# A sign bit cleared on ScalarE, one addition of epsilon, and other positions for helper work in a fused attention and experts kernel

## Chip, cores and metric

The kernel runs on one core of one Trainium2 chip. The metric is the device time of one execution in microseconds, as the median of some runs. Of the core's engines TensorE (PE) multiplies, VectorE (DVE), ScalarE (ACT) and GpSimd (POOL) do the elementwise work, and SyncE (SP) issues all the DMAs from one queue. Each engine works its own instructions in order.

## What is computed

Three layers follow each other on 2304 tokens of width 512.

```python
# 1. linear attention: batch 4, heads 8, sequence 576, head width 64
q_s = softmax(q, axis=-1); k_s = softmax(k, axis=2)      # sums have 1e-09 added
x = q_s @ (k_s^T @ v)                                    # then (B*S, H*D) = (2304, 512)
# 2. four experts, all used, 512 -> 1024 -> 512
p = domain_probs / (domain_probs.sum(-1) + 1e-09)
x = sum_e p[:, e] * (relu(x @ w1[e]) @ w2[e])
# 3. gated layer, 512 -> 1536 -> 512; w_gate, w_val, w_out come as 64-bit floats
g = x @ w_gate
out = (g * sigmoid(g) * (x @ w_val)) @ w_out
```

## The kernel before

**Numbers.** Every operand of a large product is split into a high and a low half (`split`, L103: ScalarE rounds the high half, VectorE or GpSimd subtracts). `mm3` (L107) makes one product of three matmuls: high by high, high by low, low by high. The hidden products go by seven products of 2 x 2 blocks in place of eight (`chain`, L486; the table PRODUCTS says which of seven prepared columns `xh`, `xl` and weights go together). Between the products, ScalarE copies a bank (`snap`, L503) and VectorE adds it to another (L509, L518, L524).

**Steps.** The tokens are two halves of two batches; a half is cut into block X (512 tokens) and block Y (640 tokens). A unit is 256 hidden columns of one expert (kind "e", 32 units over both halves) or of the gated layer (kind "g", 12 units). A unit and a block make a step, 88 in all. SE = 32 is the first step of the second half's experts, SG = 64 the first gated step, SF = 76 the first gated step of the second half. In the trace step 4 begins at 122.67 us, SE at 499.64, step 36 at 558.74, SG at 893.54 and SF at 1117.68, each read from the first matmul of its weights.

**Weaving.** In step st TensorE makes the hidden block of this step (`stage_h`, 8 positions in kind "e", 14 in kind "g") and the output tiles of the step before (`stage_y`, two advances for each tile of 128 tokens: 8 for X, 10 for Y). `weave` (L754) goes from position to position: first a piece of the hidden block, then DMA stores that have come of age, then the hooks of that position, then as many advances of the output tiles as WEAVE says; what is left of the tiles goes out after the last position. The low half of the hidden block is made on VectorE (L643, L645) at the first positions of the next step.

**Hooks.** All other work hangs on pairs (step, position): the attention of the second half of the batches (`attend`, steps 2 to 29), loading and splitting weights, and these four:

- `decode` (L553) turns the 64-bit weights into 32-bit ones, half a unit's matrix at a time, 36 halves, in DRAM for later. Half n begins at eighth 51 + 12n of a step, so at position 3 and 7 in turn, from step 6 to step 58; two further stages follow two and four positions later. ScalarE scales the low words (L558); VectorE clears the sign bit of the high words (L559), clamps (L561), shifts (L563), puts the sign back (L564) and adds the low words (L566). Two buffers r take turns; the load of half n + 2 is hung behind half n.
- `save_x` (L401), by the table SAVE: TensorE turns the 128 x 128 blocks of a finished sum, ScalarE copies them, SP stores them (`sd`).
- `prepare` (L428), by PREPARE (first step after SE or SG, positions in a step, first position, distance): loads the turned sums, makes the seven columns and their halves, stores them (`pd`); READY loads the finished columns.
- `load_x` and `combine_load` (L415, L421), by LOAD_E: the same for the second half's attention result, straight from DRAM into the columns.

**What sets the order.** In step 2 and later TensorE and ScalarE keep exactly the order in which the program writes their instructions (`ordered`, L779). VectorE, GpSimd and SP get theirs from a scheduler that knows estimated durations and lets a ready instruction of a later place fill a hole. Before step 2 the scheduler orders all engines, and a written list says in which order attention pieces are emitted.

**Epsilon.** In `att_kv` the sum of the key softmax comes from a column of ones behind v, one per head (`ov[:, z, D:]`). Both columns of ones give the same sum in every partition.

The lines of the change:

```python
for z in range(GH):                                                   # L234
    zz = slice(z * D, (z + 1) * D)
    nc.vector.tensor_scalar_add(rs[zz], ov[zz, z, D:], EPS)
...
nc.scalar.activation(lo, lo.bitcast(U32), AF.Copy, scale=2.0 ** -29)  # L558
nc.vector.tensor_scalar(c, hi, 0x7FFFFFFF, None, ALU.bitwise_and)     # L559
```

Of the kernel before, what the change touches and what calls it, by code (L numbers as in the profile page):

```python
# [10 lines left out]
F32 = mybir.dt.float32  # L11
# [3 lines left out]
AF = mybir.ActivationFunctionType  # L15
ALU = mybir.AluOpType
# [3 lines left out]
EPS = 1e-9  # L20
# [7 lines left out]
def attention_experts_swiglu(ctx: ExitStack, tc: tile.TileContext, q, k, v, probs, w1, w2, wg, wv, wo, out):  # L28
# [12 lines left out]
    nc = tc.nc  # L41
    B, H, S, D = q.shape
# [13 lines left out]
    GH = 2  # L56
# [20 lines left out]
    def sbt(tag, shape, name, dt=F32):  # L77
        return sb.tile(shape, dt, tag=tag, name=name, bufs=BUFS[tag])
# [4 lines left out]
    def ps(tag, name):  # L83
        if tag in TURNS:
            TURNS[tag].append(TURNS[tag].pop(0))
            tag = TURNS[tag][0]
        return psp[-1].tile([P, 512], F32, tag=tag, name=name, bufs=BUFS[tag])
# [12 lines left out]
    def f32(ap):  # L100
        return ap.bitcast(F32)
# [15 lines left out]
    def store_later(dst, src):  # L117
        later.append((now[0], dst, src))
# [57 lines left out]
    def load_q(b, g, qt):  # L176
        h = slice(g * GH, (g + 1) * GH)
        nc.sync.dma_start(qt, q[b, h, 0:SM, :].rearrange("h (p c) d -> p h c d", c=C))
        nc.sync.dma_start(rests[b, g][RQ], q[b, h, SM:S, :].rearrange("h r d -> r h d"))
        qin[b, g] = (qt, rests.pop((b, g)))  # L180
# [3 lines left out]
    def W(z):  # L184
        return WAITS[z]

    def att_kv(b, g, tag, tag_m, tag_kv, bank):


        nm = f"{b}{g}"  # L190
        kt, vt, kr, vr = kin.pop((b, g))
        m = sbt(tag_m, [P, 2, P], f"m{nm}")
        kc = kt.rearrange("p h c d -> p c h d")
        nc.vector.tensor_tensor(m.rearrange("p c (h d) -> p c h d", h=GH), kc[:, 0:2], kc[:, 2:4], ALU.max)
        yield W(0), False
        tp = ps(bank, f"ktp{nm}")[:, :2 * P + SR]
        for c in range(2):
            nc.tensor.transpose(tp[:, c * P:(c + 1) * P], m[:, c], ident)
        nc.tensor.transpose(tp[:, 2 * P:], kr[R].rearrange("p h d -> p (h d)"), ident[R, R])
        yield W(1), True  # L200
        mx = sbt("ti", [P, 1], f"mx{nm}")
        nc.vector.tensor_reduce(mx, tp, AX.X, ALU.max)
        yield W(2), False
        mb = ps(bank, f"kmb{nm}")[:, :P]
        nc.tensor.matmul(mb, mx.to_broadcast([P, P]), ident, start=True, stop=True)
        yield W(3), True
        es = sbt(tag, [P, 2, C, GH, D], f"e{nm}") if isinstance(tag, str) else tag
        ek, eqs[b, g] = es[:, 0], es[:, 1]
        mbv = mb.rearrange("p (h d) -> p h d", h=GH)
        nc.vector.tensor_tensor(  # L210
            ek.rearrange("p c h d -> p h c d"), kt, mbv[:, :, None, :].to_broadcast([P, GH, C, D]), ALU.subtract
        )
        nc.vector.tensor_tensor(kr[R], kr[R], mbv[R], ALU.subtract)
        if (b, g) in rests:
            load_q(b, g, kt)
        nc.scalar.activation(ek, ek, AF.Exp)
        nc.scalar.activation(kr[R], kr[R], AF.Exp)
        yield W(4), False
        o = ps(bank, f"kvp{nm}")[:, :GH * D1]
        for c in range(C):  # L220
            nc.tensor.matmul(  # L221
                o, ek[:, c].rearrange("p h d -> p (h d)"), vt[:, c].rearrange("p h d -> p (h d)"),
                start=c == 0, stop=False,
            )
        nc.tensor.matmul(
            o, kr[R].rearrange("p h d -> p (h d)"), vr[R].rearrange("p h d -> p (h d)"), start=False, stop=True
        )
        yield W(5), True
        rs = sbt("ti", [P, 1], f"rs{nm}")
        ov = o.rearrange("p (z e) -> p z e", z=GH)  # L230
        kk = sbt(tag_kv, [P, 2, P], f"kk{nm}", F32R)
        kh, kl = kk[:, 0], kk[:, 1]
        nc.gpsimd.memset(f32(kk), 0.0)
        for z in range(GH):  # L234
            zz = slice(z * D, (z + 1) * D)
            nc.vector.tensor_scalar_add(rs[zz], ov[zz, z, D:], EPS)
        nc.vector.reciprocal(rs, rs)
        for z in range(GH):
            zz = slice(z * D, (z + 1) * D)
            nc.scalar.activation(kh[zz, zz], ov[zz, z, 0:D], AF.Copy, scale=rs[zz])  # L240
            nc.vector.scalar_tensor_tensor(kl[zz, zz], ov[zz, z, 0:D], rs[zz], f32(kh)[zz, zz], ALU.mult, ALU.subtract)
        kvs[b, g] = (kh, kl)
        yield W(6), False
# [309 lines left out]
    def decode(n):  # L553
        what, f, z = DEC[n]
        r = r64.pop(n)
        rv = r[:, 0:2 * NE].rearrange("p (n b) -> p n b", b=2)
        lo, hi, c = rv[:, :, 0], rv[:, :, 1], r[:, 2 * NE:]
        nc.scalar.activation(lo, lo.bitcast(U32), AF.Copy, scale=2.0 ** -29)  # L558
        nc.vector.tensor_scalar(c, hi, 0x7FFFFFFF, None, ALU.bitwise_and)  # L559
        cf = c.bitcast(F32)  # L560
        nc.vector.tensor_scalar(cf, cf, LEAST, MOST, ALU.max, ALU.min)  # L561
        yield
        nc.vector.tensor_scalar(c, c, 3, 0x3FFFFFF8, ALU.logical_shift_left, ALU.bitwise_and)  # L563
        nc.vector.scalar_tensor_tensor(c, hi, -0x40000000, c, ALU.bitwise_and, ALU.bitwise_or)  # L564
        yield
        nc.vector.tensor_tensor(c, c, lo, ALU.add)  # L566
        if (what, f) not in w32:
            w32[what, f] = dram.tile([P, 2 * NE], F32, tag=f"w32_{what}{f}", name=f"w32_{what}{f}")
        store_later(w32[what, f][:, z * NE:(z + 1) * NE], cf)
        yield  # L570
# [142 lines left out]
    def store(hf, t, src):  # L713
# [9 lines left out]

    END = {"e": 7, "g": 13}
    WEAVE = {
        "e": [0, 0, 2, 2, 2, 1, 2],
        "end": [0, 0, 0, 10],
        "g": [0, 0, 0, 0, 2, 0, 0, 0, 0, 0, 2, 2, 10, 13],
    }


# [2 lines left out]


    SAVE = [
        [[(-1, 1), (-1, 3), (-1, 5), (0, 1)], [(2, 1), (2, 3), (2, 5), (2, 7)]],
        [[(-1, 1), (-1, 3), (-1, 4), (0, 0)], [(1, 2), (1, 4), (1, 7), (1, 11)]],
    ]

    LOAD_E = [[(-3, 20), (-2, 3), (-2, 7)], [(-2, 7), (-1, 3), (-1, 6)], [(-1, 6), (0, 3), (0, 6)], [(0, 6), (1, 2), (1, 5)]]

    PREPARE = [[5, 8, 0, 4], [3, 14, 0, 2]]

    READY = [
        [[(-3, 1), (-3, 2), (-3, 3), (-3, 4), (-3, 5), (-3, 6), (-3, 7)], [(-1, 1), (-1, 2), (-1, 3), (-1, 4), (-1, 5), (-1, 6), (-1, 7)]],
# [20 lines left out]
    def at(step, pos, fn, *a):  # L767
        plan.setdefault(step, {}).setdefault(pos, []).append((fn, a))
# [14 lines left out]
    if True:  # L783
# [41 lines left out]
        def start(n):  # L825
            dec[n] = decode(n)
            next(dec[n])
# [6 lines left out]
        for n in range(len(DEC)):  # L834
            z = DEC0 + n * DEC1
# [30 lines left out]
        for z, (b, j) in enumerate(((X, 0), (X, 1), (Y, 0), (Y, 1))):  # L866
            ld, *sums = [(SE + d, pos) for d, pos in LOAD_E[z]]
            at(*ld, load_x, b, j, xd)
            for p in sums:
                at(*p, combine_load, b, j)  # L870
        for hf, (st, n, z0, dz) in enumerate(PREPARE):
            gens = [prepare(hf, b, j) for b in (X, Y) for j in range(2)]
# [163 lines left out]
```

## Time and profile before

| | |
|---|---|
| median of 3 runs | 1337.72 us (1336.94 to 1338.19) |
| profiled execution | 1339.92 us, span in the profile 1338.1 us |
| busy, share of the span | PE 96%, DVE 72%, ACT 45%, POOL 42% |
| mean granted TensorE clock | 0.983 of full speed |

An engine's busy time counts its instructions' durations; matmuls overlap, so a busy TensorE says only that it always had one under way. In the timelines the first number is the start in us from the span's start, the second the duration in us; the bracket behind an instruction gives the time that its engine had stood idle before it, and the instruction or DMA that ended this. In the groups the numbers behind the bar are the busy time in us, the mean duration of one in ns, and the idle time of the engine just before instructions of the group.

### The profile page before, as it was taken

The page shows a single profiled execution, that of the slowest core. Times are in us where ns is not written, and L with a number is a line of the kernel's source. Part 1 is how long each engine was busy: PE and PEld are TensorE (multiplying, and loading weights), DVE is VectorE, ACT ScalarE, POOL GpSimd, SP SyncE. Part 2 cuts the span into 40 slices and gives each one's busy share as a digit, 9 for nine tenths or more (in the row PEclk, how much of TensorE's full clock was granted, in tenths as well). Part 3 has the DMA queues.
Part 4 walks back from the last instruction along what each step waited for, and adds up shares of the span by engine and source line. Part 5 has one row for each costly group of instructions (what it writes and reads, how often), then busy time and mean ns, then how long its engine had stood idle before and what let it go on. Part 6 is the DMA issues. An engine that isn't in the chain of part 4 may idle for free.

```text
span 1338.1 us, 20294 instructions
## 1 busy us (share of the span) xinstructions
PE 1284.3 (96%) x7568; PEld 1147.2 (86%) x7568; DVE 966.3 (72%) x1634; ACT 598.1 (45%) x1316; POOL 562.8 (42%) x587
## 2 busy tenths in 40 slices
PE   5889999999999998999999999999999999999998
PEld 3678888888888887888888888898988899999997
DVE  6886778778778889677787877555677766666665
ACT  4654334444344444434444343345444544444442
POOL 4753433443254435443545434353444444333420
PEclk9689999999999999999999999999999999999999
DMA  9311423433323334134444432463144247111102
GB/s 206 86 54 40 148 74 102 130 96 92 113 95 112 107 113 157 69 135 129 145 145 154 131 107 72 150 208 117 64 163 155 97 137 254 55 48 48 48 1 71
DMA packets 111298, 148.15 MB, mean 111 GB/s; under 512 B 30560, under 2 KB 71520, under 8 KB 111200
## 3 DMA queue, kind: packets, MB, share of 16 engines
q1 hardware_dynamic: 111200, 146.87, 34.8%
q8 instruction: 59, 0.97, 0.3%
q14 instruction: 39, 0.32, 0.1%
HBM read 109.09 MB, written 37.75 MB: 110 GB/s over the span
## 4 chain that ended last, share of the span: by engine, by line
PE 78%; DVE 10%; DMA 5%; ACT 2%; issue 2%; SPq 1%; POOL 1%; DVEq 0%; POOLq 0%; ACTq 0%
PE o L693 11%; PE o L695 11%; PE o L694 11%; PE h L109 7%; PE h L110 7%; PE h L111 7%; PE h_1g L109 2%; PE h_1g L111 2%; PE h_1g L110 2%; PE h_1v L109 2%; PE h_1v L110 2%; PE h_1v L111 2%; DMA r<-in_moe_w_gate_dram 2%; PE kvp L221 2%; PE h_0v L109 1%
## 5 line engine op out<-in xcount | busy, mean ns | idle before, releaser
L693 PE MATMUL o<-oh,hh 128*128 128x512 f32 x792 | 315.7, 399 | 3.0 <-DVE acc L704 1.5
L695 PE MATMUL o<-oh,hl 128*128 128x512 f32 x792 | 314.6, 397 | 2.5 <-DVE hl L643 2.3
L694 PE MATMUL o<-ol,hh 128*128 128x512 f32 x792 | 312.4, 394 | 0.0
L704 DVE SCALAR_TENSOR_TENSOR acc<-o,pn,acc 128x512 f32<-128x512 f32 x270 | 200.6, 745 | 73.2 <-PE o L695 72.5
L503 ACT COPY sn<-h 128x256 f32<-128x256 f32 (+1 forms) x192 | 76.2, 397 | 253.0 <-PE h L111 252.4
L695 PEld LDWEIGHTS o<-oh,hl 128*128 128x128 f32 x792 | 148.9, 188 | 39.6 <-DVE hl L643 4.2
L638 ACT ACTIVATE hh<-g 128x512 fp32r<-128x512 f32 (+1 forms) x176 | 119.4, 686 | 130.7 <-DVE g L524 73.5
L693 PEld LDWEIGHTS o<-oh,hh 128*128 128x128 f32 x792 | 149.1, 188 | 22.6 <-DVE acc L704 1.7
L694 PEld LDWEIGHTS o<-ol,hh 128*128 128x128 f32 x792 | 148.9, 188 | 17.2
L643 DVE SCALAR_TENSOR_TENSOR hl<-g,hh 128x512 fp32r<-128x512 f32 (+1 forms) x128 | 109.2, 855 | 31.5 <-ACT hh L638 28.7
L708 DVE TENSOR_TENSOR acc<-o,acc 128x512 f32<-128x512 f32 x90 | 61.9, 688 | 45.9 <-PE o L695 44.8
L521 ACT COPY g<-h 128x256 f32<-128x256 f32 (+1 forms) x64 | 25.6, 400 | 89.4 <-PE h L111 89.3
L645 DVE TENSOR_TENSOR hl<-g,hh 128x512 fp32r<-128x512 f32 (+1 forms) x48 | 48.6, 1012 | 3.2 <-ACT hh L638 2.4
L559 DVE TENSOR_SCALAR r<-r 128x512 int32<-128x512 int32 x36 | 23.1, 642 | 30.6 <-DMA r<-in_moe_w_val_dram 11.7
L105 POOL TENSOR_TENSOR xo<-xp,xo 128x256 fp32r<-128x256 f32 (+1 forms) x24 | 22.4, 935 | 52.5 <-ACT xo L104 47.2
L662 ACT ACTIVATE g<-g 128x512 f32<-128x512 f32 (+1 forms) x48 | 33.0, 688 | 21.0 <-DVE g L524 21.0
L524 DVE TENSOR_TENSOR g<-h,sn 128x256 f32<-128x256 f32 (+1 forms) x64 | 29.0, 453 | 17.9 <-PE h L111 17.5
L503 ACT COPY sn_1g<-h_1g 128x320 f32<-128x320 f32 x36 | 15.4, 427 | 56.2 <-PE h_1g L111 56.1
L518 DVE TENSOR_TENSOR g<-h,sn 128x256 f32<-128x256 f32 (+1 forms) x64 | 28.9, 451 | 9.7 <-ACT sn L503 9.5
L566 DVE CUSTOM_DVE_ANT_0 r<-r 128x1024 uint16<-128x1024 uint16 x36 | 32.0, 889 | 3.1 <-ACT r L558 3.0
L509 DVE TENSOR_TENSOR g<-h,sn 128x256 f32<-128x256 f32 (+1 forms) x64 | 28.8, 451 | 3.7 <-PE h L111 2.3
L564 DVE SCALAR_TENSOR_TENSOR r<-r 128x512 int32<-128x512 int32 x36 | 31.0, 862 | 0.7
(1174 smaller groups left out, 3857.1 us busy)
## 6 DMA issues: line engine op xcount, KB each, us to landing
pd<-xo SPq DMA_DIRECT2D x28, 320.0 KB, 2.8
pd<-xo SPq DMA_DIRECT2D x28, 256.0 KB, 2.5
r<-in_moe_w_gate_dram SPq DMA_DIRECT2D x12, 512.0 KB, 4.3
r<-in_moe_w_val_dram SPq DMA_DIRECT2D x12, 512.0 KB, 4.6
r<-in_moe_w_out_dram SPq DMA_DIRECT2D x12, 512.0 KB, 4.0
xl<-pd SPq DMA_DIRECT2D x14, 320.0 KB, 5.3
xh<-pd SPq DMA_DIRECT2D x14, 320.0 KB, 5.3
out_dram<-acc SPq DMA_DIRECT2D x16, 256.0 KB, 2.3
```

Of the source, the lines that this page charges most:

```text
L109: nc.tensor.matmul(o, wh, xh, start=first, stop=False, skip_group_check=more)
L110: nc.tensor.matmul(o, wh, xl, start=False, stop=False, skip_group_check=more)
L111: nc.tensor.matmul(o, wl, xh, start=False, stop=last, skip_group_check=more)
L503: nc.scalar.copy(sn[z], banks[0])
L638: nc.scalar.activation(hh[:, :, t * n:(t + 1) * n], g[:, :, t], AF.Relu if kind == "e" else AF.Copy)
L643: nc.vector.scalar_tensor_tensor(hl[:, :, ts], g[:, :, t], 0.0, f32(hh[:, :, ts]), ALU.max, ALU.subtract)
L645: nc.vector.tensor_tensor(hl[:, :, ts], g[:, :, t], f32(hh[:, :, ts]), ALU.subtract)
L693: nc.tensor.matmul(p, hh[:, z, ts], w[z][0], start=z == 0, stop=False)
L694: nc.tensor.matmul(p, hh[:, z, ts], w[z][1], start=False, stop=False)
L695: nc.tensor.matmul(p, hl[:, z, ts], w[z][0], start=False, stop=z == NF - 1)
L704: nc.vector.scalar_tensor_tensor(o, p, weight, o, ALU.mult, ALU.add)
L708: nc.vector.tensor_tensor(o, p, o, ALU.add)
```

## The change

Four things are edited. In `att_kv` the two additions of epsilon, one per head on 64 partitions, become one on 128 partitions that reads the first head's column of ones. In `decode` the sign bit is cleared by ScalarE, as an activation Abs on the high words read as floats, in place of VectorE's bitwise AND; it stands behind L558 on ScalarE. WEAVE lets kind "e" advance the output tiles three times at position 6 instead of twice, and kind "g" nine times at position 12 instead of ten. SAVE, LOAD_E and PREPARE get other positions.

```diff
--- before.py
+++ after.py
@@ -231,9 +231,7 @@
         kk = sbt(tag_kv, [P, 2, P], f"kk{nm}", F32R)
         kh, kl = kk[:, 0], kk[:, 1]
         nc.gpsimd.memset(f32(kk), 0.0)
-        for z in range(GH):
-            zz = slice(z * D, (z + 1) * D)
-            nc.vector.tensor_scalar_add(rs[zz], ov[zz, z, D:], EPS)
+        nc.vector.tensor_scalar_add(rs, ov[:, 0, D:], EPS)
         nc.vector.reciprocal(rs, rs)
         for z in range(GH):
             zz = slice(z * D, (z + 1) * D)
@@ -556,8 +554,8 @@
         rv = r[:, 0:2 * NE].rearrange("p (n b) -> p n b", b=2)
         lo, hi, c = rv[:, :, 0], rv[:, :, 1], r[:, 2 * NE:]
         nc.scalar.activation(lo, lo.bitcast(U32), AF.Copy, scale=2.0 ** -29)
-        nc.vector.tensor_scalar(c, hi, 0x7FFFFFFF, None, ALU.bitwise_and)
         cf = c.bitcast(F32)
+        nc.scalar.activation(cf, hi.bitcast(F32), AF.Abs)
         nc.vector.tensor_scalar(cf, cf, LEAST, MOST, ALU.max, ALU.min)
         yield
         nc.vector.tensor_scalar(c, c, 3, 0x3FFFFFF8, ALU.logical_shift_left, ALU.bitwise_and)
@@ -723,9 +721,9 @@
 
     END = {"e": 7, "g": 13}
     WEAVE = {
-        "e": [0, 0, 2, 2, 2, 1, 2],
+        "e": [0, 0, 2, 2, 2, 1, 3],
         "end": [0, 0, 0, 10],
-        "g": [0, 0, 0, 0, 2, 0, 0, 0, 0, 0, 2, 2, 10, 13],
+        "g": [0, 0, 0, 0, 2, 0, 0, 0, 0, 0, 2, 2, 9, 13],
     }
 
 
@@ -734,13 +732,13 @@
 
 
     SAVE = [
-        [[(-1, 1), (-1, 3), (-1, 5), (0, 1)], [(2, 1), (2, 3), (2, 5), (2, 7)]],
-        [[(-1, 1), (-1, 3), (-1, 4), (0, 0)], [(1, 2), (1, 4), (1, 7), (1, 11)]],
+        [[(-1, 1), (-1, 2), (-1, 5), (0, 3)], [(2, 2), (2, 4), (2, 5), (2, 7)]],
+        [[(-1, 1), (-1, 3), (0, 4), (0, 0)], [(1, 2), (1, 6), (1, 5), (1, 12)]],
     ]
 
-    LOAD_E = [[(-3, 20), (-2, 3), (-2, 7)], [(-2, 7), (-1, 3), (-1, 6)], [(-1, 6), (0, 3), (0, 6)], [(0, 6), (1, 2), (1, 5)]]
-
-    PREPARE = [[5, 8, 0, 4], [3, 14, 0, 2]]
+    LOAD_E = [[(-3, 20), (-2, 3), (-2, 7)], [(-2, 7), (-1, 3), (-1, 5)], [(-1, 6), (0, 3), (0, 6)], [(0, 4), (1, 2), (1, 5)]]
+
+    PREPARE = [[3, 8, 0, 4], [5, 14, 1, 2]]
 
     READY = [
         [[(-3, 1), (-3, 2), (-3, 3), (-3, 4), (-3, 5), (-3, 6), (-3, 7)], [(-1, 1), (-1, 2), (-1, 3), (-1, 4), (-1, 5), (-1, 6), (-1, 7)]],
```

## Rows read from the trace of the kernel before

**Rows 1.** Page, part 1: busy time of each engine, share, instructions.

```profile
PE 1284.3 (96%) x7568; PEld 1147.2 (86%) x7568; DVE 966.3 (72%) x1634; ACT 598.1 (45%) x1316; POOL 562.8 (42%) x587
```

**Rows 2.** Page, part 4: the chain that ended last, by engine.

```profile
PE 78%; DVE 10%; DMA 5%; ACT 2%; issue 2%; SPq 1%; POOL 1%; DVEq 0%; POOLq 0%; ACTq 0%
```

**Rows 3.** By stretch: length, busy PE, PEld, DVE, ACT, POOL, clock, DMA share, GB/s.

```profile
122.67:499.64 376.97, 368.88 (x2138) 325.87 (x2138) 299.47 (x531) 162.05 (x355) 160.26 (x171) 0.99 0.34 103
499.64:558.74 59.10, 53.07 (x301) 46.22 (x300) 47.15 (x68) 27.62 (x58) 26.75 (x23) 0.97 0.41 134
558.74:893.54 334.80, 333.88 (x1946) 298.84 (x1945) 242.66 (x385) 141.03 (x301) 148.95 (x141) 1.00 0.41 132
893.54:1117.68 224.14, 215.56 (x1357) 198.20 (x1356) 151.32 (x235) 110.61 (x244) 97.95 (x93) 0.99 0.41 139
1117.68:1338.10 220.42, 216.44 (x1364) 199.51 (x1362) 138.58 (x212) 93.89 (x199) 68.55 (x66) 1.00 0.17 60
```

**Rows 4.** Timeline, PE: start, duration, instruction, [idle before it <- what ended it].

```profile
162.16 0.46 PE L205 MATMUL kmb<-ident,mx 128*128 128x128 f32 x2 [2.03 <-DVE qT L105]
...
349.86 0.46 PE L205 MATMUL kmb<-ident,mx 128*128 128x128 f32 x2 [2.98 <-DVE qT L105]
...
490.87 0.50 PE L693 MATMUL o<-oh,hh 128*128 128x512 f32 x1 [1.46 <-DVE acc L704]
...
517.98 0.79 PE L695 MATMUL o<-oh,hl 128*128 128x512 f32 x1 [2.02 <-DVE hl L643]
...
759.04 0.39 PE L109 MATMUL h<-xh,wh26a 128*128 128x256 f32 x1 [0.73 <-DVE g L518]
```

**Rows 5.** Groups of instructions by shape: busy us, mean ns | idle before.

```profile
L566 DVE CUSTOM_DVE_ANT_0 r<-r 128x1024 uint16<-128x1024 uint16 x36 | 32.0, 889 | 3.1 <-ACT r L558 3.0
...
L564 DVE SCALAR_TENSOR_TENSOR r<-r 128x512 int32<-128x512 int32 x36 | 31.0, 862 | 0.7
L561 DVE TENSOR_SCALAR r<-r 128x512 f32<-128x512 f32 x36 | 26.6, 738 | 0.5
L558 ACT ACTIVATE r<-r 128x512 int32<-128x512 uint32 x36 | 24.2, 672 | 0.0
L559 DVE TENSOR_SCALAR r<-r 128x512 int32<-128x512 int32 x36 | 23.1, 642 | 30.6 <-DMA r<-in_moe_w_val_dram 11.7 <-DMA r<-in_moe_w_gate_dram 10.9 <-DMA r<-in_moe_w_out_dram 8.0
L563 DVE TENSOR_SCALAR r<-r 128x512 int32<-128x512 int32 x36 | 21.4, 594 | 0.5
```

**Rows 6.** Timeline, DVE: same columns.

```profile
160.26 0.43 DVE L559 TENSOR_SCALAR r<-r 128x512 int32<-128x512 int32 x1 [1.14 <-DMA r<-in_moe_w_val_dram]
...
335.16 0.82 DVE L643 SCALAR_TENSOR_TENSOR hl<-g,hh 128x640 fp32r<-128x640 f32 x1
...
345.14 1.31 DVE L559 TENSOR_SCALAR r<-r 128x512 int32<-128x512 int32 x1 [1.20 <-DMA r<-in_moe_w_out_dram]
...
348.36 0.69 DVE L564 SCALAR_TENSOR_TENSOR r<-r 128x512 int32<-128x512 int32 x1
```

**Rows 7.** Timeline, ACT: same columns.

```profile
334.87 0.67 ACT L558 ACTIVATE r<-r 128x512 int32<-128x512 uint32 x1
335.43 0.36 ACT L503 COPY sn<-h 128x256 f32<-128x256 f32 x1
...
377.39 0.66 ACT L558 ACTIVATE r<-r 128x512 int32<-128x512 uint32 x1
```

**Rows 8.** Waits of ACT, steps 4 to 63: us in total, times, longest.

```profile
ACT sn L503 <- PE h L111: 235.5, 137, 3.6
```

**Rows 9.** Groups by shape, the addition of epsilon.

```profile
L236 DVE TENSOR_SCALAR rs<-kvp 64x1 f32<-64x1 f32 x32 | 5.0, 155 | 7.0 <-PE kvp L225 6.5
```

**Rows 10.** Timeline, ACT and PE, step 70.

```profile
1015.55 0.46 ACT L104 CAST xo<-xp 128x320 fp32r<-128x320 f32 x1 [3.77 <-DVE xp L441]
...
1016.33 0.58 PE L109 MATMUL h_0g<-xh,wh35a 128*128 128x256 f32 x1 [2.87 <-ACT sn_0g L503]
```

**Rows 11.** Timeline, ACT, step 64.

```profile
902.37 1.28 ACT L662 ACT_TABLE_LOAD   x1
```

## Prediction

> **What bounds the kernel now.** I read the page's first part, then the chain of waits, then the table by stretch, then TensorE's own waits, and only then VectorE's and ScalarE's rows beside each wait. TensorE is busy 96% of the span [rows 1] and the chain that ended last runs 78% through it [rows 2]: VectorE's 72% and ScalarE's 45% matter only where one of their instructions comes last and TensorE stands. The table by stretch says how much that is [rows 3]. Span less PE busy is 8.1 us in steps 4 to 31 (377.0 - 368.9), 6.0 in steps 32 to 35, 0.9 in steps 36 to 63, 8.6 in steps 64 to 75 and 4.0 from step 76 on, mostly the tail. So 24 us between 123 and 1118 us are all that better placed helper work can win there; the rest is matmuls, which the change leaves alone. The reader should see in [rows 4] that single waits of 0.7 to 3.0 us make up the idle time, and that they end with a VectorE instruction.
>
> **Decoding: the sign bit moves to ScalarE.** There are 36 decodes, each now of one ScalarE conversion (L558, 0.67 us) and five VectorE instructions [rows 5]. What the change removes on VectorE is L559: 36 x 0.642 = 23.1 us busy. More important is the 30.6 us that VectorE stood before it, until the load of r had landed: VectorE works its queue in order, so everything behind L559 stood too. The worst place shows it [rows 6]: at 345.14 L559 has waited 1.20 us for the load, and L559 to L564 then hold VectorE until 349.05; behind them is the low half of a turned block, for whose bank TensorE waits 2.98 us, until 349.86 [rows 4]. At 160.26 the wait of 1.14 and L559's 0.43 are 1.57 of the 2.03 us that TensorE stood until 162.16. The waits at 490.87 (1.46) and 759.04 (0.73) end with a VectorE instruction that stood behind the same decode instructions. Sum: 2.98 + 1.57 + 1.46 + 0.73 = 6.7 us of TensorE's idle time made by early decodes. Smaller ones I leave out.
>
> After the change the first VectorE instruction of a decode (L561) needs Abs, and Abs stands in ScalarE's fixed order right behind L558. L558 comes late: for the load used at 345.14, it runs at 377.39 [rows 7], 32 us after L559, when the load has long landed. So VectorE can no longer stand for a load; those four stalls lose their cause. In return L561, L563, L564 and L566 (0.738 + 0.594 + 0.862 + 0.889 = 3.1 us, [rows 5]) come in one lump behind Abs, where only L566 came before. What that costs isn't in the trace; its nearest rows are today's 36 lumps of L559 to L564 (0.642 + 0.738 + 0.594 + 0.862 = 2.8 us), which cost 6.7 us. Lower end 0: steps 36 to 63 hold 14 lumps beside 0.9 us of idle time [rows 3]. Upper end here 7.4: the same 6.7, times 3.1 / 2.8. I take 3.2, a little under the middle, since the lump starts when ScalarE says so and not when a load lands. Net: 6.7 - 3.2 = 3.5 us gained, ends +0.7 lost and 6.7 gained.
>
> Abs itself has no row. L558 reads and writes the same shape with the same stride in 0.672 us, so I take that: 36 x 0.672 = 24.2 us more on ScalarE. Who waits behind it is the next snapshot copy (L503), then VectorE's addition. In steps 4 to 63 ScalarE stood 235.5 us in 137 waits, 1.7 us each, for TensorE before L503 [rows 8]; Abs goes into such a hole, and I cost it at nothing. With that cover gone it is 0.67 us each. In the tightest spot, a decode begun at position 7, L558 starts at 334.87, the snapshot follows at 335.43 [rows 7], and two more products and two half output tiles pass before TensorE adds into that bank again. The r buffer comes free some 3 us later, so its next load too; with 32 us between landing and L558 nothing waits for that, and the store of the decoded half, queued on SP ahead of that load, is needed 250 us later or more.
>
> [...]
>
> **Epsilon.** Two additions on 64 partitions become one on 128: 32 of 0.155 us become 16 [rows 9]. That is 16 x 0.155 = 2.5 us of VectorE; ScalarE's scaling waits for it, but no wait of TensorE in the trace ends with L236 or L237. I take 0.5, ends 0 and 2.5.
>
> **Positions.** The tenth half tile of a Y block now goes out at position 6, ahead of position 7's hooks, instead of after them; in the 349.86 case that puts 0.7 us of matmuls ahead of the waiting one. It overlaps the gain above and I count nothing. The "g" entry changes nothing: 2 + 2 + 2 + 9 = 15 advances still exhaust the at most 11 of a step. Saves: their 36 transposes a half stay, with ScalarE's copies and SP's stores; most move by one or two positions, one by a whole step, within the stretches that idle 6.0 and 8.6 us. LOAD_E moves one sum by one position and one load by two; SP stands before that load today until a sum frees its buffer, so it won't go earlier. The first PREPARE begins two steps earlier, on steps 35 and 36, right behind the saves of step 34. I take 0 for these, ends 3 lost and 3 gained, half of the 6.0.
>
> The second PREPARE moves from steps 67 to 72 to steps 69 to 74, and from even to odd positions. Nearly all of the 8.6 us there is its doing: from step 76 on, without it, there is almost none before the tail [rows 3]. The largest: ScalarE stands 3.77 us for a subtraction of the preparation, and TensorE 2.87 us for the snapshot queued behind [rows 10]. The shift keeps parity of the step (X on X), so the same meetings recur, with 1 position more for VectorE or a load. I take 1.0 gained; ends 3 lost, 7 gained. SP's pd stores and xp loads move along as a block, and the loads of finished columns (READY) still begin two steps behind X's last store and one behind Y's.
>
> **Sum.** -3.5 - 0.5 - 0 - 1.0 = -5.0 us. On the profiled execution 1339.92 - 5.0 = 1334.9. Its 1339.92 lies 2.2 above the median 1337.72, so the forecast for the median is 1332.7. Own range of this case: 1329 to 1335.
>
> **Rivals.**
> (a) Stalls only move. The lump of 3.1 us costs what the early decodes cost: +7.4 - 6.7 = +0.7, with epsilon 0 to -0.5 and the rest nothing: 1338. For it: VectorE is 79% busy in steps 4 to 31 [rows 3]. Against: no load ends its waits any more. Chance 0.22.
> (b) The preparation's stalls go as well: -5.0 and another 6 of the 8.6: 1326.7. For it: the 3.77 us hang on one meeting of queues [rows 10]. Against: same parity. Chance 0.13.
> (c) Slower: half of the decodes begin at position 7, and their lump falls into the first positions of the next step, where VectorE makes the low half of the hidden block. If it goes in front, the output matmuls wait as they do at 517.98, 2.02 us [rows 4]. It decides from 5.0 / 2.02, some three of 18 decodes; with six, 1332.7 + 12.1 = 1344.8. Against: at 335.16 the last low half starts 0.3 us after L558 [rows 6], before Abs would end at 336.2. Chance 0.14.
> (d) Abs isn't in the function table that is loaded. The trace shows a table load of 1.28 us where Silu first comes [rows 11], and none between ReLU, Copy and Exp. Worst case two per decode: 72 x 1.28 = 92 us, 1425. Chance 0.01. [...]
>
> **How the numbers follow.** The forecast has 0.50; it is the likeliest, so 1332.7. Range 1326 to 1341: it takes in (b), (a) and the weak end of (c). Faster by over 0.2% (2.7 us, about what a measurement of this kernel can tell from no change) are 0.49 of the forecast and (b): 0.62. Within 0.2% is (a): 0.22. Slower are (c), (d) and 0.01 of the forecast for an order of the start that falls badly, since fewer instructions there can reorder it all: 0.16.
>
> **What would show it.** VectorE's waits for r's loads gone; L561 just after Abs; TensorE's waits at the places of [rows 4] gone and none of over 1 us with L561 to L566 in front; ScalarE's waits before L503 shorter by about 24 us; steps 69 to 74 idle about as long as 67 to 72 do now. The forecast falls if TensorE's idle time in steps 4 to 31 stays near 8.1, if Abs takes far over 0.67 us, or if a snapshot behind Abs releases TensorE.

## The result, and the profile after

The changed kernel takes 1323.46 us (median of 4 executions, 1322.12 to 1325.43), the kernel before beside it 1337.45. The ratio is 0.9889, its 95% interval 0.9865 to 0.9913: 14.0 us gained as the medians have it, 11.6 to 18.1 by the interval. The forecast was 1332.7 with a range of 1326 to 1341: the right side, far too little. The profiled execution took 1322.43 us, 17.5 less than the one profiled before; its span is 1320.7.

From the addition of epsilon on, the line numbers of the changed kernel are two lower: L556 is now the scaling of the low words, L558 is Abs, L559 the clamp, L561 the shift, L562 the sign, L564 the addition, L501 the snapshot. First the page, parts 1 and 4 [rows 1, 2 before]:

```profile
PE 1276.5 (97%) x7568; PEld 1144.3 (87%) x7568; DVE 941.4 (71%) x1582; ACT 617.6 (47%) x1352; POOL 563.3 (43%) x587
...
PE 85%; DVE 5%; POOL 3%; issue 2%; SPq 2%; DMA 1%; ACT 1%; POOLq 0%; DVEq 0%; ACTq 0%
```

VectorE lost 25 us of work and ScalarE gained 20, but the line to look at is the chain: VectorE's share of it fell from 10% to 5%, DMA's from 5% to 1%. The table by stretch, cut at the same steps as [rows 3] (steps 4 to 31, 32 to 35, 36 to 63, 64 to 75, the rest; length, busy PE, PEld, DVE, ACT, POOL, clock, DMA share, GB/s), says where the time went:

```profile
121.44:485.62 364.18, 363.94 (x2138) 323.39 (x2138) 278.33 (x495) 171.69 (x374) 158.79 (x172) 1.00 0.34 106
485.62:544.01 58.39, 52.72 (x302) 46.13 (x300) 47.79 (x70) 28.79 (x61) 27.31 (x23) 0.97 0.43 135
544.01:878.11 334.10, 333.14 (x1942) 298.54 (x1940) 241.13 (x376) 149.34 (x315) 149.54 (x141) 1.00 0.40 132
878.11:1100.23 222.12, 215.52 (x1362) 198.79 (x1361) 149.47 (x235) 111.39 (x245) 97.77 (x93) 0.99 0.42 140
1100.23:1320.70 220.47, 216.41 (x1364) 199.51 (x1362) 138.49 (x212) 93.80 (x199) 68.54 (x66) 1.00 0.18 60
```

Steps 4 to 31 went from 376.97 to 364.18 us, 12.8 of the profiles' 17.5. The rest: 1.2 before step 4, 0.7 in each of the next two stretches, 2.0 in steps 64 to 75. In steps 4 to 31 two things vanished. Idle time of TensorE fell from 8.1 to 0.2 us (364.18 - 363.94). And TensorE's busy time, for the same 2138 matmuls, fell from 368.88 to 363.94: 4.9 us. The clock column has most of the reason, 0.99 before and 1.00 now: part of the matmuls had run at a granted clock of 0.50 of full speed (from 163 to 166 us, for one). The part on the prediction shows where.

The decode's groups by shape (busy us, mean ns | idle before) answer to [rows 5]:

```profile
L562 DVE SCALAR_TENSOR_TENSOR r<-r 128x512 int32<-128x512 int32 x36 | 35.5, 987 | 0.3
...
L564 DVE CUSTOM_DVE_ANT_0 r<-r 128x1024 uint16<-128x1024 uint16 x36 | 29.0, 805 | 0.3
...
L556 ACT ACTIVATE r<-r 128x512 int32<-128x512 uint32 x36 | 24.0, 667 | 0.0
L558 ACT ACTIVATE r<-r 128x512 f32<-128x512 f32 x36 | 23.8, 661 | 0.0
...
L559 DVE TENSOR_SCALAR r<-r 128x512 f32<-128x512 f32 x36 | 19.3, 536 | 3.4 <-ACT r L558 3.1
...
L561 DVE TENSOR_SCALAR r<-r 128x512 int32<-128x512 int32 x36 | 18.2, 505 | 0.5
```

VectorE's 30.6 us before the first instruction of a decode are 3.4 now, and no DMA is among the releasers. Abs takes 0.661 us, where L558's 0.672 was forecast. The step in which TensorE had waited 2.98 us (the end of step 20), timelines of ScalarE and VectorE:

```profile
328.92 0.66 ACT L556 ACTIVATE r<-r 128x512 int32<-128x512 uint32 x1
329.21 0.81 DVE L641 SCALAR_TENSOR_TENSOR hl<-g,hh 128x640 fp32r<-128x640 f32 x1
329.47 0.66 ACT L558 ACTIVATE r<-r 128x512 f32<-128x512 f32 x1
330.17 0.43 DVE L559 TENSOR_SCALAR r<-r 128x512 f32<-128x512 f32 x1
...
330.51 0.42 DVE L507 TENSOR_TENSOR g<-h,sn 128x256 f32<-128x256 f32 x1
...
330.84 0.42 DVE L561 TENSOR_SCALAR r<-r 128x512 int32<-128x512 int32 x1
...
331.17 0.69 DVE L105 TENSOR_TENSOR ol<-raw10o,oh 128x512 fp32r<-128x512 f32 x1
...
334.15 0.68 DVE L564 CUSTOM_DVE_ANT_0 r<-r 128x1024 uint16<-128x1024 uint16 x1
```

The lump, as the forecast called the VectorE instructions of a decode behind Abs, runs from 330.17 to 334.83, behind Abs and behind the low half of the hidden block (329.21), in a stretch in which TensorE doesn't wait. It isn't one block: other work of VectorE goes in between, here a sum (L507) and a split (L105) among others, and in all 36 decodes of this trace one to nine instructions between the clamp and the addition. What is left of TensorE's longer waits, in its timeline:

```profile
489.81 0.50 PE L693 MATMUL o<-oh,hl 128*128 128x512 f32 x1 [1.44 <-DVE hl L641]
...
499.52 0.55 PE L109 MATMUL h<-xh,wh16a 128*128 128x256 f32 x1 [2.47 <-DVE g L516]
...
514.49 0.39 PE L109 MATMUL h<-xh,wh17a 128*128 128x256 f32 x1 [1.20 <-DVE g L516]
...
560.16 0.50 PE L693 MATMUL o<-oh,hl 128*128 128x512 f32 x1 [0.96 <-DVE hl L641]
...
999.72 0.41 PE L109 MATMUL h_1g<-xh,wh35a 128*128 128x320 f32 x1 [1.37 <-ACT g L519]
...
1034.13 0.39 PE L109 MATMUL h_0g<-xh,wh36a 128*128 128x256 f32 x1 [2.59 <-ACT sn_0g L501]
```

None lies in steps 4 to 31. The last one is the meeting of [rows 10], 2.87 us then, two steps later now.

### The profile page after: what moved, and what is told of

Same layout as the page of the kernel before. It is cut to its first block, busy times and chain, and to the rows that moved or that the text cites. A ratio compares the mean times of both kernels' runs of the same rounds, so it can differ in the third digit from the quotient of the medians.

```text
span 1320.7 us, 20275 instructions
## 1 busy us (share of the span) xinstructions
PE 1276.5 (97%) x7568; PEld 1144.3 (87%) x7568; DVE 941.4 (71%) x1582; ACT 617.6 (47%) x1352; POOL 563.3 (43%) x587
## 4 chain that ended last, share of the span: by engine, by line
PE 85%; DVE 5%; POOL 3%; issue 2%; SPq 2%; DMA 1%; ACT 1%; POOLq 0%; DVEq 0%; ACTq 0%
PE o L691 13%; PE o L693 13%; PE o L692 13%; PE h L109 9%; PE h L110 8%; PE h L111 8%; PE h_1g L109 2%; PE h_1g L110 2%; PE h_1g L111 2%; PE h_1v L109 2%; PE h_1v L110 2%; PE h_1v L111 2%; PE h_0v L109 1%; PE h_0v L111 1%; PE h_0v L110 1%
## 5 line engine op out<-in xcount | busy, mean ns | idle before, releaser
L693 PE MATMUL o<-oh,hl 128*128 128x512 f32 x792 | 313.9, 397 | 2.4 <-DVE hl L641 2.4
L501 ACT COPY sn<-h 128x256 f32<-128x256 f32 (+1 forms) x192 | 76.3, 397 | 244.4 <-PE h L111 244.0
L693 PEld LDWEIGHTS o<-oh,hl 128*128 128x128 f32 x792 | 149.1, 188 | 38.9 <-DVE hl L641 3.3
L636 ACT ACTIVATE hh<-g 128x512 fp32r<-128x512 f32 (+1 forms) x176 | 119.3, 685 | 105.2 <-DVE g L522 51.7
L641 DVE SCALAR_TENSOR_TENSOR hl<-g,hh 128x512 fp32r<-128x512 f32 (+1 forms) x128 | 118.7, 929 | 34.1 <-ACT hh L636 30.7
L706 DVE TENSOR_TENSOR acc<-o,acc 128x512 f32<-128x512 f32 x90 | 61.9, 688 | 46.9 <-PE o L693 45.9
L643 DVE TENSOR_TENSOR hl<-g,hh 128x512 fp32r<-128x512 f32 (+1 forms) x48 | 47.9, 999 | 4.0 <-ACT hh L636 3.2
L516 DVE TENSOR_TENSOR g<-h,sn 128x256 f32<-128x256 f32 (+1 forms) x64 | 29.0, 453 | 16.6 <-ACT sn L501 16.4
L501 ACT COPY sn_1g<-h_1g 128x320 f32<-128x320 f32 x36 | 15.4, 427 | 53.0 <-PE h_1g L111 53.0
L105 POOL TENSOR_TENSOR xo<-xp,xo 128x256 fp32r<-128x256 f32 (+1 forms) x24 | 22.5, 939 | 40.2 <-ACT xo L104 39.0
L562 DVE SCALAR_TENSOR_TENSOR r<-r 128x512 int32<-128x512 int32 x36 | 35.5, 987 | 0.3
L672 DVE TENSOR_TENSOR g<-g,v 128x512 f32<-128x512 f32 (+1 forms) x24 | 22.9, 956 | 10.7 <-ACT v L519 10.6
L507 DVE TENSOR_TENSOR g<-h,sn 128x256 f32<-128x256 f32 (+1 forms) x64 | 28.7, 448 | 1.6 <-ACT wh2a L104 0.9
L104 ACT CAST xo<-xp 128x256 fp32r<-128x256 f32 (+1 forms) x56 | 24.3, 434 | 11.1 <-DMA xp<-sd 5.1
```

Source lines behind the costliest of these rows:

```text
L501: nc.scalar.copy(sn[z], banks[0])
L636: nc.scalar.activation(hh[:, :, t * n:(t + 1) * n], g[:, :, t], AF.Relu if kind == "e" else AF.Copy)
L641: nc.vector.scalar_tensor_tensor(hl[:, :, ts], g[:, :, t], 0.0, f32(hh[:, :, ts]), ALU.max, ALU.subtract)
L643: nc.vector.tensor_tensor(hl[:, :, ts], g[:, :, t], f32(hh[:, :, ts]), ALU.subtract)
L693: nc.tensor.matmul(p, hl[:, z, ts], w[z][0], start=False, stop=z == NF - 1)
L706: nc.vector.tensor_tensor(o, p, o, ALU.add)
```

## Experiments

The theory: a decode that VectorE took up early stood for a load and held what lay behind it; behind Abs it begins when all is there. The rivals: VectorE is simply relieved of 23 us; or the new positions did it. The table gives all kernels that were executed several times: ratio to the kernel before, measured beside it, with 95% interval, and the stretches of the one profiled execution in us. Experiment 8 was executed once and has no ratio.

| kernel | ratio | steps 4 to 31 | 32 to 35 | 36 to 63 | 64 to 75 |
|---|---|---|---|---|---|
| before | 1 | 377.0 | 59.1 | 334.8 | 224.1 |
| changed | 0.9889 (0.9865 to 0.9913) | 364.2 | 58.4 | 334.1 | 222.1 |
| 1 Abs alone | 0.9897 (0.9867 to 0.9926) | 366.9 | 58.9 | 333.1 | 226.2 |
| 2 epsilon alone | 0.9995 (0.9979 to 1.0011) | 377.1 | 59.3 | 335.2 | 225.7 |
| 3 positions alone | 0.9960 (0.9931 to 0.9989) | 374.9 | 56.8 | 337.0 | 222.7 |
| 4 WEAVE alone | 0.9985 (0.9969 to 1.0000) | 374.6 | 59.1 | 334.9 | 225.6 |
| 5 late AND | 0.9914 (0.9888 to 0.9939) | 366.4 | 59.2 | 333.5 | 224.2 |
| 6 Abs twice | 0.9917 (0.9888 to 0.9945) | 365.6 | 61.4 | 334.5 | 222.9 |
| 7 longer lump | 0.9977 (0.9961 to 0.9993) | 369.0 | 61.9 | 339.8 | 222.0 |
| 9 pause | 0.9920 (0.9893 to 0.9947) | 364.2 | 58.8 | 332.7 | 227.6 |
| 10 pause, spread | 0.9910 (0.9882 to 0.9938) | 364.2 | 60.2 | 332.7 | 226.0 |
| 11 old SAVE, LOAD_E | 0.9897 (0.9866 to 0.9929) | 365.2 | 59.4 | 334.5 | 223.4 |
| 12 old PREPARE | 0.9876 (0.9833 to 0.9920) | 364.2 | 58.8 | 332.7 | 224.0 |

Executions of one kernel spread by 0.2 to 1.0% from the fastest to the slowest, so differences of 2 us between two of these are told by a stretch and its waits, not by the ratio. A stretch is one execution too: where it holds waits of 2 us or so, it can differ by 2 us of busy time between executions, as experiments 9 and 10 show (51.95 and 54.40 us in steps 32 to 35).

**1. Abs alone.**

```diff
-        nc.vector.tensor_scalar(c, hi, 0x7FFFFFFF, None, ALU.bitwise_and)
         cf = c.bitcast(F32)
+        nc.scalar.activation(cf, hi.bitcast(F32), AF.Abs)
```

> The kernel before with Abs on ScalarE in place of VectorE's AND, nothing else. Theory (decodes that stand for a load make TensorE's waits, and each wait of 2 us or more also lowers the granted clock for a while after it): steps 4 to 31 shrink from 377.0 to about 365 us, their granted clock goes from 0.99 to 1.00, and the whole is 10 to 13 us faster, some 1325 to 1327. Rival (the positions did it, above all the tenth half tile): steps 4 to 31 stay above 373 us and the whole within 4 us of the kernel before.

1.0% faster, 13.8 us by the ratio, as much as the whole change within the intervals. Its row for steps 4 to 31:

```profile
121.71:488.62 366.91, 365.40 (x2139) 323.10 (x2138) 282.39 (x506) 171.23 (x372) 158.87 (x171) 1.00 0.35 106
```

Idle time 1.5 us, clock 1.00: 10.1 of the 12.8 us are Abs. The rival that the positions did it falls for this stretch.

**2. Epsilon alone.** The three lines of the loop become the one line, nothing else.

> The kernel before with the single addition of epsilon, nothing else. Theory: 0 to 1.5 us faster, all of it before step 4, since the first step after the change begins 1.2 us earlier. Rival (the fewer instructions also move VectorE's decodes off the two long waits in steps 7 and 20): these two waits of 2.0 and 3.0 us go and the whole is over 5 us faster.

No difference that can be measured. The two waits of 2.0 and 3.0 us in steps 7 and 20 stand as before, so the reordered start doesn't move the decodes.

**3 and 4. All positions alone; WEAVE alone.** The new tables SAVE, LOAD_E, PREPARE and WEAVE; then only

```diff
-        "e": [0, 0, 2, 2, 2, 1, 2],
+        "e": [0, 0, 2, 2, 2, 1, 3],
-        "g": [0, 0, 0, 0, 2, 0, 0, 0, 0, 0, 2, 2, 10, 13],
+        "g": [0, 0, 0, 0, 2, 0, 0, 0, 0, 0, 2, 2, 9, 13],
```

> The kernel before with the new tables (output tiles at position 6, saves, loads of columns, preparation), nothing else. Theory: steps 4 to 31 stay within 2 us of 377.0 apart from the 0.7 us that the half tile puts into the wait of step 20; steps 64 to 75 go from 224.1 to about 222; the whole 2 to 4 us faster. Rival (the positions took the waits away): over 8 us faster with steps 4 to 31 below 370.

> The kernel before with the tenth half tile at position 6 and nine advances in place of ten at position 12 of gated steps, nothing else. Theory: within 1.5 us of the kernel before; the wait of step 20 is 0.7 us shorter. Rival: this edit alone takes the waits in steps 20 and 7 away and is over 5 us faster.

The positions alone give 0.4% (0.1 to 0.7), WEAVE alone 0.15% (0 to 0.31). Beside Abs they add less than that (0.9889 against 0.9897 for Abs alone); both shorten the same two waits. With WEAVE alone the wait of step 20 is still there, 0.6 us shorter, about the half tile that now goes ahead of it. TensorE's timeline there, and the table by stretch around it:

```profile
350.80 0.46 PE L205 MATMUL kmb<-ident,mx 128*128 128x128 f32 x2 [2.36 <-DVE qT L105]
```

```profile
338.00:353.00 15.00, 12.64 (x73) 10.55 (x71) 11.30 (x16) 4.32 (x10) 8.19 (x10) 1.00 0.46 152
```

In this execution the clock was 1.00 in the 15 us around a wait of 2.36 us; in the one of before it was 0.86 in the 12 us around one of 2.03. So the idle time is 8.1 us in both (374.59 - 366.50 here), and the stretch is 2.4 us shorter.

**5. The AND stays on VectorE, but late.** ScalarE writes one column that the AND then overwrites, so the AND has to come after it; VectorE's work stays.

```diff
-        nc.vector.tensor_scalar(c, hi, 0x7FFFFFFF, None, ALU.bitwise_and)
+        nc.scalar.copy(c.bitcast(F32)[:, 0:1], ident[:, 0:1]); nc.vector.tensor_scalar(c, hi, 0x7FFFFFFF, None, ALU.bitwise_and)
```

> The kernel before with the AND left on VectorE, but made to wait: ScalarE first writes one column of c right behind L558, and the AND overwrites it. VectorE's work stays what it was, all five instructions of a decode now come behind ScalarE. Theory (the place in the queue counts, not the 23 us of work moved): VectorE's waits for r's loads are gone, steps 4 to 31 take 365 to 369 us in place of 377 (366.9 with Abs alone), the whole is 8 to 13 us faster. Rival (VectorE is relieved of work): steps 4 to 31 stay above 374 us, the whole within 4 us of the kernel before.

This tells the theory from relief. The AND's group and the stretch of steps 4 to 31:

```profile
L559 DVE TENSOR_SCALAR r<-r 128x512 int32<-128x512 int32 x36 | 21.4, 594 | 6.1 <-ACT r L559 5.0 <-DMA pd<-xo 1.0
```

```profile
120.16:486.61 366.45, 364.72 (x2139) 323.72 (x2139) 289.16 (x523) 163.28 (x372) 160.35 (x171) 1.00 0.35 106
```

VectorE still does all five instructions of a decode, and no longer waits for r's loads (6.1 us of idle time in place of 30.6). Steps 4 to 31 take 366.4 us, as with Abs alone (366.9). The gain is the place in the queue; the 23 us of work taken off VectorE are worth nothing that shows, though the intervals of the two ratios leave room for some us. What the experiment doesn't separate is the standing for a load and the early decode's own work: at the wait that ended at 349.86, VectorE had stood 1.20 us for the load and then worked 3.9 us on L559 to L564 [rows 6], and the late AND takes both away.

**6. Abs twice.** One more line `nc.scalar.activation(cf, hi.bitcast(F32), AF.Abs)` in the changed kernel.

> The changed kernel with Abs done twice, the same values, 36 x 0.67 = 24 us more on ScalarE. Theory (Abs stands in holes before the snapshots): within 3 us of the changed kernel (ratio to before 0.987 to 0.992), steps 36 to 63 within 1 us of 334. Rival (ScalarE's queue is nearly full at these places): 36 times up to 0.67 us, the whole 10 us or more slower than the changed kernel, near 1335, with snapshots among the releasers of TensorE in steps 6 to 59.

24 us more on ScalarE cost 1.4 us in steps 4 to 31 and 0.4 in steps 36 to 63, against up to 24 if each had been in the way: it stands in holes, as the forecast said. Steps 32 to 35 lost 3.0, where a wait of 2 us and more was already; 2.0 of them are busy time (54.74 against 52.72), at a clock of 0.94 in place of 0.97. The whole is 3.7 us slower than the changed kernel by the two ratios, whose intervals overlap: a little over the theory's 3 us, inside the ratios that it gave, and far from the rival's 10.

**7. A longer lump.** The clamp three times, so the lump is 3.9 us by the groups above (2.83 + 2 x 0.536) in place of 2.8; by this kernel's own groups it is 4.0.

```diff
         nc.vector.tensor_scalar(cf, cf, LEAST, MOST, ALU.max, ALU.min)
+        nc.vector.tensor_scalar(cf, cf, LEAST, MOST, ALU.max, ALU.min)
+        nc.vector.tensor_scalar(cf, cf, LEAST, MOST, ALU.max, ALU.min)
```

> The changed kernel with the clamp done three times, the same values: the lump behind Abs grows from 3.1 to about 4.4 us, VectorE does 36 x 2 x 0.5 to 0.74 = 36 to 53 us more. Theory (the scheduler places the lump in holes as long as it knows when it can begin): within 3 us of the changed kernel. Rival (the forecast's 3.2 us for the lump, by its length): a lump half as long again costs at least 3 us more, with waits of TensorE behind L561 to L566 in steps 4 to 31.

The theory falls. Most of the gain is gone: 4.8 us in steps 4 to 31, 3.5 in steps 32 to 35, 5.7 in steps 36 to 63, where one wait of 0.96 us had stood. The last of these, and the waits of steps 4 to 63 (us in total, times, longest; L516 is the same line as in the changed kernel, L643 and L695 are its L641 and L693):

```profile
553.35:893.18 339.83, 336.12 (x1942) 299.50 (x1940) 258.28 (x408) 149.34 (x315) 150.45 (x141) 0.99 0.40 131
```

```profile
PE h L109 <- DVE g L516: 7.2, 6, 4.9
PE o L695 <- DVE hl L643: 4.2, 3, 2.3
```

So the lump is nearly free at its length, and at 1.4 times its length no longer. With the late AND in it (experiment 5) it is 3.5 us by its groups there, and steps 36 to 63 hold 0.2 us of idle time (333.48 - 333.28): the limit lies between, as far as these two kernels can be compared, which differ in their tables too. Whether the length of the lump or the 40 us more work of VectorE (981.68 against 941.40) makes the waits wasn't separated. The first wait is VectorE's addition behind the lump, the second the low half of the hidden block: the mechanism of the forecast's rival (c), at a longer lump.

**8. What a wait costs.** Copies on ScalarE at position 2 of five X steps of the changed kernel, 8, 12, 16, 20 and 24 of them; ScalarE keeps the program's order, so its snapshots come late and TensorE stands, 2.1 to 7.6 us, in a stretch that is otherwise free of waits.

```diff
+        for n, st in enumerate((38, 42, 46, 50, 54)):
+            for _ in range(8 + 4 * n):
+                at(st, 2, nc.scalar.copy, idle, ident[:, 0:1].to_broadcast([P, 256]))
```

> The changed kernel with 8, 12, 16, 20 and 24 copies of 128 x 256 more on ScalarE at position 2 of steps 38, 42, 46, 50 and 54, about 0.27 us each: ScalarE's snapshots come 2.2 to 6.5 us later and TensorE stands. It measures what a wait of TensorE costs beside its own length. Theory: where TensorE stands 2 us or more, its granted clock falls to half in the matmuls behind, and the step grows by up to 1.7 us more than the wait; short waits cost their length alone. Rival (the clock follows something else): each step, 11.92 us without, grows by its wait alone and the granted clock stays 1.00.

The first and the third of these waits in TensorE's timeline, with matmuls ahead of and behind the third:

```profile
580.97 0.39 PE L109 MATMUL h<-xh,wh19a 128*128 128x256 f32 x1 [2.11 <-ACT sn L501]
...
681.67 0.39 PE L692 MATMUL o<-ol,hh 128*128 128x512 f32 x1
681.90 0.40 PE L693 MATMUL o<-oh,hl 128*128 128x512 f32 x1
686.69 0.58 PE L109 MATMUL h<-xh,wh23a 128*128 128x256 f32 x1 [4.39 <-ACT sn L501]
...
688.13 0.63 PE L691 MATMUL o<-oh,hh 128*128 128x512 f32 x1
688.56 0.63 PE L692 MATMUL o<-ol,hh 128*128 128x512 f32 x1
```

Ahead of the wait two matmuls of 512 columns start 0.23 us apart, behind it 0.43. The pair of steps around the first, third and last wait, and the first pair in the changed kernel without copies:

```profile
573.09:600.89 27.80, 25.69 (x139) 22.43 (x138) 18.91 (x30) 14.85 (x33) 11.04 (x10) 0.94 0.37 114
...
676.52:706.98 30.46, 26.07 (x140) 23.01 (x138) 16.38 (x29) 16.99 (x39) 11.75 (x11) 0.89 0.38 122
...
788.23:822.44 34.21, 26.57 (x139) 23.47 (x138) 15.16 (x25) 19.25 (x44) 9.47 (x9) 0.85 0.17 54
```

```profile
568.91:592.82 23.91, 23.91 (x139) 21.20 (x138) 18.84 (x30) 11.80 (x25) 11.03 (x10) 1.00 0.39 132
```

A wait of 2.1 us made its pair 3.9 us longer (27.80 - 23.91): 2.1 idle, and 1.8 more of busy time for the same matmuls at a clock of 0.94. For the third and the last the busy time grew by 2.4 and 2.9 us (26.07 and 26.57 against 23.70, the busy time of each of the later pairs in the changed kernel). The theory holds in its first part, and for the longer waits its "up to 1.7" is too small. Its second part, that short waits cost their length alone, is not tested here: the shortest wait was 2.11 us.

**9 and 10. No decodes in steps 31 to 34; the preparation spread as well.** Changed kernel with the decodes from the 18th on four steps later, then also with the second preparation from step 66 at every third position.

```diff
-            z = DEC0 + n * DEC1
+            z = DEC0 + n * DEC1 + (32 if n > 16 else 0)
```

```diff
-    PREPARE = [[3, 8, 0, 4], [5, 14, 1, 2]]
+    PREPARE = [[3, 8, 0, 4], [2, 14, 3, 3]]
```

> The changed kernel with the decodes from the 18th on four steps later, so that none falls into steps 31 to 34, where the saves and the loads of columns also want VectorE. Theory (the lump does cost where VectorE is full, and a wait of 2 us or more lowers the clock besides): the waits of 1.4, 2.5 and 1.2 us at 488 to 514 us go or shrink, steps 32 to 35 take 54 to 56 us in place of 58.4, the whole is 2 to 6 us faster than the changed kernel, 1318 to 1321. Rival (these waits belong to the loads of columns alone, as before the change): steps 32 to 35 stay at 58 to 59 us and the whole within 2 us.

> As the kernel with the pause, and the second preparation from step 66 on at every third position in place of from step 69 at every second. Theory (its waits come from sums and copies that stand too close on two queues): steps 64 to 75 go from 222 to 217 to 220 us, and the whole is 2 to 5 us faster than with the pause alone. Rival (they come from the first positions of a step, wherever the preparation lies): 221 to 224 us, no gain.

Both theories fall. Without decodes there, steps 32 to 35 take 58.8 and 60.2 us, no less than the 58.4 of the changed kernel, and waits of 2.37 and 2.69 us for the same two VectorE instructions stay. Ahead of them VectorE's timeline has the sums and splits of the loaded columns, so they belong to these in the main, as the first rival has it; its time for the whole isn't met, since by the ratios the kernel with the pause is 4.1 us slower than the changed one. The rows of steps 32 to 35, first with the pause, then with the pause and the spread preparation, show one thing more:

```profile
489.16:547.93 58.77, 51.95 (x301) 44.87 (x300) 42.11 (x58) 25.60 (x55) 26.56 (x23) 1.00 0.30 96
...
485.68:545.86 60.18, 54.40 (x302) 47.83 (x301) 41.36 (x58) 25.80 (x55) 26.20 (x23) 0.94 0.29 94
```

The same two waits passed at full clock in the first and not in the second (1.00 against 0.94), and the busy time differs by 2.4 us. Step 37 loses its wait (332.7 in steps 36 to 63). Behind, the pause costs: in steps 64 to 75 new waits appear for the weights of the first gated unit, shown here from the waits of TensorE in that stretch of the kernel with the pause:

```profile
PE h_0g L111 <- POOL wl32a L105: 2.2, 2, 1.7
...
PE h_0g L109 <- ACT wh32a L104: 1.1, 1, 1.1
```

The decodes now end at step 62 instead of 58, and those weights' preparation comes late; whether through SP's queue or VectorE's wasn't separated. In steps 64 to 75, with the preparation spread as well, the wait behind a load of turned sums (1.37 us in the changed kernel, at 999.72; 1.46 with the pause) is gone and others have come: 226.0 us against 227.6, over the 221 to 224 of the second rival. So no gain that shows.

**11 and 12. The old SAVE and LOAD_E; the old PREPARE,** each in the changed kernel.

> The changed kernel with SAVE and LOAD_E of before. Theory (these two tables matter little): within 3 us of the changed kernel; steps 32 to 35 at 58 to 61 us. Rival (they earn what the two parts together have over Abs alone): 3 to 5 us slower than the changed kernel.

> The changed kernel with PREPARE of before. Theory (the same meetings recur two steps later): steps 64 to 75 take 222 to 226 us in place of 222, the whole 0 to 4 us slower than the changed kernel, and step 37 loses its 1.1 us. Rival: over 5 us slower, with a further wait of 2 us or more in steps 64 to 75.

Neither is told apart from the changed kernel by its ratio. By stretches, one execution each: the old SAVE and LOAD_E cost 1.0 us in each of steps 4 to 31 and 32 to 35 and 1.3 in steps 64 to 75. The old PREPARE gives back 1.4 us in steps 36 to 63 (the wait at 560.16 is gone) and costs 1.9 in steps 64 to 75. No kernel here beats the changed one clearly.

## Why the prediction was wrong, point by point

The main mechanism was right: a decode's place in VectorE's queue, and not its work, made the waits. In the decode's term one size was wrong, one term was missing, and small waits were left out.

**The decode's gain.** The step "6.7 - 3.2 = 3.5" failed; steps 4 to 31 gained 12.8 us, 10.1 with Abs alone. First, the lump was put at 3.2 us, a middle between 0 and what today's lumps cost. It cost 0 to 1: 0.2 us of idle time is left in steps 4 to 31, and one wait of 0.96 us stands at 560.16, which the old PREPARE takes away too. The lower end was right. The forecast had costed one block of VectorE's time, and other work goes in between (shown above); experiment 7 shows that this has a limit: at 1.4 times the length, the gain of 14 us goes down to 3. Second, a term was missing. The working took a wait of TensorE at its own length. But behind the two longest of the waits that went, 2.03 and 2.98 us, the clock of the kernel before had fallen (columns as in [rows 3]):

```profile
160.00:172.00 12.00, 9.97 (x50) 9.03 (x50) 8.39 (x18) 3.15 (x7) 1.47 (x3) 0.86 0.46 125
...
349.00:360.00 11.00, 10.14 (x52) 9.32 (x53) 6.43 (x15) 3.67 (x8) 1.08 (x1) 0.84 0.40 129
```

In the rest of steps 4 to 31 it was 1.00. An estimate from the two rows is 0.14 x 12 + 0.16 x 11 = 3.4 us lost; experiment 8 has 1.8 us for one such wait, and with Abs alone the busy time fell by 3.5 (368.88 to 365.40). The other 1.5 of the 4.9 us of busy time went only when the other edits joined Abs, and no run says why. Third, four waits of 6.7 us were counted, of which one, 0.73 us at 759.04, lies behind step 31, and smaller ones were left out; in the end 7.9 us of idle time went in steps 4 to 31. By sizes: 7.9 + 4.9 = 12.8, where 3.5 stood.

The forecast also took idle time for all that better placed helper work can win. That failed for the same reason: in steps 4 to 31, with 8.1 us of it, 12.8 were won. Idle time doesn't hold what the clock loses behind a wait; the busy time of the matmuls does (368.88 us before, 363.94 after). The clock column of [rows 3] showed 0.99, and 1% of 377 us is about the 3.4 us that were overlooked.

**Abs at nothing.** Right. ScalarE's waits before the snapshot, in us, times and longest, were 235.5 in [rows 8]; after:

```profile
ACT sn L501 <- PE h L111: 227.4, 141, 3.6
```

They shrank by 8 and not by the 24 us that the forecast gave as its sign. ScalarE's waits for VectorE before the high half of the hidden block (L638, now L636) shrank as well, from 73.5 to 51.4 us; whether Abs stands there or VectorE comes earlier wasn't separated. No snapshot behind Abs releases TensorE in steps 4 to 31, and experiment 6 shows the room. The durations of Abs and of the AND decide nothing here: Abs takes 0.661 us and the AND took 0.642, and with the AND left on VectorE, but late, the time is the same within the intervals.

**Epsilon.** 0.5 forecast, no measurable difference alone. The 1.2 us before step 4 can't be put down to it: step 4 begins at 120.6 to 125.0 us in the nine traces with the one addition and at 120.2 to 125.6 in the five with two. So the 0.5 is neither shown nor refuted.

**Positions.** Counted at nothing but for the second PREPARE. WEAVE's half tile went ahead of the waiting matmul as worked out (0.6 us, forecast 0.7). The tables together are worth 1.5 to 9 us alone, by their interval, more than the 1.0 that stood; beside Abs most of that is taken already. The second PREPARE gave 2.0 us in steps 64 to 75 (1.9 by experiment 12), forecast 1.0. That this is no scatter is seen over all traces whose decodes keep their steps: 224.0 to 226.2 us in the six with the old position, 221.6 to 223.4 in the six with the new one. And the same meeting came back two steps later as said: ScalarE's wait for a sum of the preparation, with the snapshot behind it.

```profile
1033.35 0.46 ACT L104 CAST xo<-xp 128x320 fp32r<-128x320 f32 x1 [3.38 <-DVE xp L439]
```

The first PREPARE, put at 0 together with the saves and loads, cost 1.4 us by experiment 12.

**The rivals.** (a), stalls only move: no; that needs a longer lump. (b), the preparation's stalls go too: no, 6.6 us of 8.6 are left. (c), the lump ahead of the low half: hardly at this length; the 0.96 us at 560.16 are such a wait. (d), a table load per decode: none. In the trace ScalarE's second and last load of a table is still Silu's:

```profile
887.36 1.28 ACT L660 ACT_TABLE_LOAD   x1
```

Of the signs that the forecast named, one more failed in a small way: at 514.49 TensorE's wait of 1.20 us has the clamp in front, 0.41 us of it.

The range was too narrow at its fast end. That end, 1326, came from rival (b), which didn't happen; the decode's own upper end, 6.7, was a bound of idle time and lay below the 10.1 us that Abs alone gained in steps 4 to 31.

## What to carry to other kernels

An instruction that waits for a load holds up what lies behind it on VectorE, however little it does (VectorE stood 30.6 us before 36 ANDs of 0.642 us, and 6.1 with the late AND): hang it behind something that comes long after the landing, and let it find its inputs there. Where TensorE bounds, price a wait of 2 us or more at up to 2 or 3 us above its length (1.8 to 2.9 in experiment 8, and in some executions nothing, as at the 2.36 us of experiment 4), and read the clock column and the busy time of the same matmuls as well as the idle time. Measure how much longer a burst may be before it stops being free; here 1.4 times its length was too much.

## What the hardware showed

In the trace of the kernel before, TensorE's granted clock was 0.50 of full speed in each microsecond from 163 to 166, behind the wait that ended at 162.16, and 1.00 from 166.5 to 172. From 163.36 on matmuls of 320 columns start 0.27 us apart, and from 166.46 on 0.15, while TensorE works on. In experiment 8 matmuls of 512 columns start 0.43 us apart behind a wait of 4.39 us and 0.23 ahead of it; 1.8 us were lost behind the wait of 2.1 and 2.9 behind the longest, 7.6. The clock did not fall behind every wait. Counted over steps 4 to 75 of all fourteen traces, it fell at 4 of 53 waits of 1 to 2 us (the shortest 1.53 us, in experiment 2), at 27 of 40 waits of 2 to 3 us and at all four longer ones, and nowhere else. A wait of 2.36 us passed at full clock in experiment 4 (1.00 from 338 to 353 us), and the same waits of 2.37 and 2.69 us passed at full clock in experiment 9 and not in experiment 10 (1.00 and 0.94 in steps 32 to 35). There the busy time of the same stretch was 51.95 and 54.40 us; how much of the scatter between executions of one kernel comes from it wasn't measured.

VectorE's durations went with GpSimd's work. The clamp, 36 times the same shape, took 0.41 to 0.43 us in the 19 places of the changed kernel's trace where GpSimd had no instruction under way, and 0.41 to 1.51 us in the other 17, with all seven above 0.6 us among them. In the kernel before, where the forecast took its mean of 0.738 us [rows 5], the free ones are 13, again of 0.41 to 0.43 us, and 19 of the other 23 are above 0.6. So the group's mean, 0.738 us before and 0.536 after, went with what GpSimd did meanwhile. That GpSimd is the cause, no run here isolates.
